# Attention scores by half-array matmuls, q loaded in long rows, and a new planned order

## The chip, the cores and the metric

The kernel runs on one core of a Trainium2 chip. The metric is the device time of one execution in microseconds (us). The core has five engines that run side by side and wait for one another through semaphores: TensorE (PE in the profile; PEld is its weight load), VectorE (DVE), ScalarE (ACT), GpSimd (POOL) and SyncE (SP), which here issues all transfers between HBM and the on-chip memory SBUF. Matmul results go to PSUM, which PE, DVE and ACT reach.

## The reference, cut to what matters

```python
# q, k, v: (2, 8, 576, 64), fp32
scores = scale * np.matmul(q, k.transpose(0, 1, 3, 2))
mask = (rel >= 0) & (rel < 64)             # rel = query position - key position
attn = softmax(np.where(mask, scores, -1e9))
x = (attn @ v) as (1152, 512)
# first expert layer
h = x @ w_in                               # 512 -> 2048
g = np.maximum(h, 0.0) + np.log1p(np.exp(-np.abs(h)))
x = g @ w_out                              # 2048 -> 512
# second expert layer: four experts, each token a weighted sum of all
p = domain_probs / (domain_probs.sum(-1, keepdims=True) + 1e-09)
out = sum over e of p[:, e] * (np.maximum(x @ w1[e], 0.0) @ w2[e])
```

## The kernel before, in words

**Attention.** The 1152 tokens are cut into 18 groups of 64 queries; because of the window of 64, a group sees 128 keys. Heads go in four pairs (NP = 4): 128 SBUF partitions hold the 64 dimensions of the one head and of the other. Three groups form a chunk, whose keys (kT), queries (qz) and values come by transfers from SP (`load_qk`, `load_v`). The score matmul (`scores_pe`, L957 to L962) takes the two heads of a pair in one go: qz holds, for each pair, 128 columns, the first 64 with the first head's queries in the upper 64 rows and zeros below, the last 64 with the second head's queries in the lower rows and zeros above. So a matmul over all 128 rows adds only zeros from the other head. The zeros are written once by DVE (`zeros`, L1022) into two qz buffers; the loads then fill the other halves with two transfers for each chunk (L858), in runs of 64 floats.

The rest of a group: DVE adds the mask and takes the row maximum (L968), ACT takes the exponentials and their sums (L972), DVE the reciprocals (`one_over`, L976 and L977), one of the engines scales the probabilities (L980 or L984), PE transposes them (L989), a copy brings them to SBUF (pT, L249 or L253), PE multiplies with v (L1001, on half of the output columns at a time), and two operations write x as a high and a low part (L249 or L253, then L1013).

**First expert layer.** 16 chunks of 128 hidden columns, in four units of four, over three blocks of 384 tokens: 48 steps. A step is twelve matmuls into h (L468), the softplus on ACT, DVE and POOL (L487 to L505; l minus w; then g's high part and its low part, both through the helper lines L249, L253 and L268), and twelve matmuls that add to acc (L538). Weights come as 64-bit floats and are turned into a high and a low fp32 part by a chain on ACT and DVE (`convert`, L391 to L415).

**Second expert layer.** Two pairs of token halves (2 x 320 and 2 x 256), 16 weight quads each: seven half products a quad (L703), sums (L724), relu in two parts (L768, L772), and the second matmuls (L798). The weight sums S and the token sums T run through L268.

**What sets the order.** Nothing is written out by hand. Each operation is an `Op` with a duration for each engine that may do it, what it comes after, and a due time. `plan()` (L177) works the due times back from the matmul steps, then goes through modelled time: it takes the operation that can start earliest, among those the most urgent, and picks its engine. The letters `E_...` in `P` (L50) list the engines that may do an operation: A is ACT, D is DVE, V is DVE when it shares SBUF ports with POOL, G is POOL. Letters ending in 0 hold for the first unit or the first block of tokens: E_T copies pT, E_H writes x's high part, E_P scales, E_R rounds in the softplus, E_S subtracts w from l, E_G and E_L make g's high and low part, E_S2 and E_T2 make the sums S and T. `PE` and `PE2` (L76) model a matmul; WB, DW2 and DV shift the due times of weight conversions and loads.

Of the kernel before, what the change touches and what calls it, by code (L numbers as in the profile page):

```python
# [21 lines left out]
def kernel(  # L22
# [124 lines left out]
    class Ring:  # L147
# [10 lines left out]
        def take(self, first):  # L158
# [519 lines left out]
    def quad(n, p, e, j, due1, due2):  # L678
# [162 lines left out]
    mask = ap_.tile([128, 2, 128], F32, bufs=1, name="mask")  # L841
    qz = [ap_.tile([128, GPC, NP, 2, W], F32, bufs=1, name=f"qz{i}") for i in range(2)]
    pn = cp.tile([128, NT // 128, E], F32, name="pn")
    psum = cp.tile([128, NT // 128], F32, name="psum")

    kT, vt = {}, {}
    qk_there, v_there = {}, {}
    qk_done, v_done = {}, {}

    def load_qk(c, due):  # L850
        b, s = c // CPB, (c % CPB) * CH

        def keys(k0, k1):
            if c not in kT:
                kT[c] = ap_.tile([128, NP, W + CH], F32, tag="kT", bufs=2, name=f"kT{c}")
            nc.sync.dma_start(out=kT[c][:, :, k0:k1], in_=k[b, :, :, s - W + k0:s - W + k1].rearrange("h p s -> p h s"))

        def queries(j, g0, g1):  # L858
            rows = slice(j * D, (j + 1) * D)
            nc.sync.dma_start(out=qz[c % 2][rows, g0:g1, :, j, :], in_=q[b, rows, s // W + g0:s // W + g1])  # L860


        if s:
            parts = [(0, W + CH, 0, GPC)]
        elif b:
            parts = [(W, W + CH, 0, GPC)]
        else:
            parts = [(W, 3 * W, 0, 1), (3 * W, W + CH, 1, GPC)]
        qk_there[c], after = [], rings["kT"].next()
        for k0, k1, g0, g1 in parts:  # L870
            there = [Op({"Q": ((k1 - k0) * 0.0057, lambda k0=k0, k1=k1: keys(k0, k1))}, after, due, 2.2)]
            if g0 == 0:
                qk_done[c], after = rings["kT"].take(there[0]), []
            for j in range(2):
                there.append(Op({"Q": ((g1 - g0) * 0.364, lambda j=j, g0=g0, g1=g1: queries(j, g0, g1))},
                                [qk_done[c - 2]] if c >= 2 else (), due, 2.2))
            for g in range(g0, g1):
                qk_there[c].append(there + qk_there[c][g0 - 1] if g0 else there)
# [18 lines left out]
    class Group:  # L897
# [59 lines left out]
        def scores_pe(self):  # L957
            k0 = W * self.il if self.i else W
            self.s = self.bank(0, [128, NP, 128])
            for hp in range(NP):  # L960
                nc.tensor.matmul(self.s[:, hp, :], lhsT=qz[self.c % 2][:, self.il, hp],  # L961
                                 rhs=kT[self.c][:, hp, k0:k0 + 128], start=True, stop=True)  # L962

# [57 lines left out]

    def zeros(i):  # L1022
        for j in range(2):
            nc.vector.memset(qz[i][(1 - j) * D:(2 - j) * D, :, :, j, :], 0.0)

    def masks():
# [108 lines left out]
    for n, (p, e, j) in enumerate(quads):  # L1135
# [60 lines left out]
```

## Time and profile before

| | us |
|---|---|
| median of 3 runs | 670.98 (670.78 to 674.19) |
| the profiled execution | 672.12 |
| its span, first to last instruction | 670.3 |
| PE busy, of the span | 633.2 (94%) |
| DVE busy | 502.9 (75%) |
| ACT busy | 353.1 (53%) |
| POOL busy | 296.2 (44%) |

The profile gives for each instruction its engine, source line, start and duration, and infers what ended each wait. Lines are those of the kernel file; helper lines (L249, L253, L268) are shared by many operations, which the tile's name tells apart. The busy rows in slices are tenths of a slice of 1/40 of the span. Matmuls are pipelined, so a busy PE need not be at its best pace. Durations in groups are means over all instructions of a group.

### The profile page before, as it was taken

To read this page: it belongs to the slowest core of one execution; us is meant where nothing else is said; L and a number is where in the kernel's file an instruction comes from. 1 tells how busy PE (TensorE), PEld (TensorE's weight loads), DVE (VectorE), ACT (ScalarE), POOL (GpSimd) and SP (SyncE) were. 2 spreads that over 40 slices of the span, in tenths; PEclk is the share of its full clock that TensorE was granted. 3 is DMA by queue.
4 is the path that set the end of the run, shared out by engine and by line. 5 is a ranking of instruction groups with operands and counts; after the bars stand their busy time and mean duration, and the time that the engine had idled before them with its cause. 6 is when DMAs were issued, how large, how long until landed. Compare 5 with 4: busy or idle time off the path is not lost.

```text
span 670.3 us, 10414 instructions
## 1 busy us (share of the span) xinstructions
PE 633.2 (94%) x3864; PEld 581.8 (87%) x3864; DVE 502.9 (75%) x902; ACT 353.1 (53%) x767; POOL 296.2 (44%) x281
## 2 busy tenths in 40 slices
PE   5668999999999899799999999999998999999997
PEld 5558999989999799688989998998887889888996
DVE  5998999999999978965666474564897685766643
ACT  5998987767677576434235243332534343434330
POOL 2222623334444386564716345181745536454310
PEclk9898999999999999899999999999999999999999
DMA  8995312311112321012211321231152132223001
GB/s 233 279 252 189 119 47 81 118 73 63 65 64 66 123 64 64 0 64 75 115 64 64 117 72 64 75 114 63 64 189 79 65 126 95 95 73 116 1 1 63
DMA packets 38946, 62.81 MB, mean 94 GB/s; under 512 B 12144, under 2 KB 15216, under 8 KB 38896
## 3 DMA queue, kind: packets, MB, share of 16 engines
q1 hardware_dynamic: 38896, 62.16, 28.9%
q8 instruction: 30, 0.49, 0.3%
q14 instruction: 20, 0.16, 0.1%
HBM read 59.79 MB, written 2.36 MB: 93 GB/s over the span
## 4 chain that ended last, share of the span: by engine, by line
PE 68%; DVE 21%; ACT 4%; issue 3%; DMA 2%; POOL 1%; SPq 1%; ACTq 0%; DVEq 0%; POOLq 0%
PE acc L798 27%; PE y L703 11%; PE z L703 7%; PE x L703 7%; PE acc L538 7%; PE h L468 6%; DVE g L268 2%; PE s L961 2%; DVE w L499 2%; DMA qz<-in_q_dram 2%; DVE km L412 2%; DVE G L772 1%; DVE l L505 1%; DVE xo L268 1%; DVE kh L406 1%
## 5 line engine op out<-in xcount | busy, mean ns | idle before, releaser
L798 PE MATMUL acc<-wb,G 128*128 128x512 f32 x864 | 211.0, 392 | 3.2 <-DVE G L772 3.2
L798 PEld LDWEIGHTS acc<-wb,G 128*128 128x128 f32 x864 | 158.2, 188 | 33.8 <-DVE G L772 4.6
L538 PE MATMUL acc<-g,w 128*128 128x384 f32 x576 | 112.9, 343 | 6.3 <-DVE g L268 5.0
L268 POOL TENSOR_TENSOR l<-l,w 128x384 f32<-128x384 f32 x48 | 68.1, 1424 | 110.2 <-DVE l L505 82.5
L538 PEld LDWEIGHTS acc<-g,w 128*128 128x128 f32 x576 | 101.3, 191 | 9.5 <-DVE g L268 7.4
L468 PE MATMUL h<-x,w 128*128 128x384 f32 x576 | 106.9, 336 | 2.2 <-DVE w L415 1.4
L468 PEld LDWEIGHTS h<-x,w 128*128 128x128 f32 x576 | 99.9, 188 | 3.6 <-DVE w L415 1.7
L268 POOL TENSOR_TENSOR wc<-S,wc 128x1024 fp32r<-128x1024 f32 x16 | 38.8, 2428 | 115.4 <-ACT wc L249 115.3
L768 ACT ACTIVATE G<-C 128x320 fp32r<-128x320 f32 (+3 forms) x64 | 35.9, 561 | 78.3 <-PE acc L798 39.6
L772 DVE SCALAR_TENSOR_TENSOR G<-C,G 128x320 fp32r<-128x320 f32 (+3 forms) x64 | 51.9, 812 | 32.1 <-ACT G L768 31.9
L703 PE MATMUL z<-xo,wc 128*128 128x320 f32 (+1 forms) x384 | 62.2, 297 | 1.5 <-DVE C L724 1.1
L703 PE MATMUL y<-xo,wc 128*128 128x320 f32 (+1 forms) x384 | 63.0, 300 | 0.1
L703 PE MATMUL x<-xo,wa 128*128 128x320 f32 (+1 forms) x384 | 61.6, 296 | 0.8 <-ACT p L249 0.5
L268 POOL TENSOR_TENSOR S<-rq 128x256 f32<-128x256 f32 x64 | 55.0, 866 | 13.9 <-DVE wc L268 8.5
L703 PEld LDWEIGHTS x<-xo,wa 128*128 128x128 f32 x384 | 56.2, 189 | 3.5 <-ACT p L249 0.8
L249 ACT ACTIVATE wa<-rq 128x512 fp32r<-128x512 f32 x64 | 31.1, 516 | 53.3 <-PE y L703 53.2
L703 PEld LDWEIGHTS y<-xo,wc 128*128 128x128 f32 x384 | 56.2, 192 | 2.7 <-DVE q L724 0.7
L703 PEld LDWEIGHTS z<-xo,wc 128*128 128x128 f32 x384 | 54.8, 190 | 2.2 <-DVE C L724 1.3
L268 POOL TENSOR_TENSOR wa<-rq,wa 128x256 fp32r<-128x256 f32 (+1 forms) x25 | 31.6, 1270 | 56.0 <-ACT wa L249 53.4
L249 ACT ACTIVATE wc<-S 128x1024 fp32r<-128x1024 f32 x32 | 33.7, 1052 | 32.2 <-PE z L703 30.3
L268 DVE TENSOR_TENSOR wb<-rq,wb 128x1024 fp32r<-128x1024 f32 x27 | 36.1, 1337 | 6.3 <-ACT wb L249 5.0
L249 ACT ACTIVATE wb<-rq 128x1024 fp32r<-128x1024 f32 x32 | 33.5, 1047 | 13.8 <-PE acc L798 13.8
(83 smaller groups left out, 986.2 us busy)
## 6 DMA issues: line engine op xcount, KB each, us to landing
rq<-in_moe_w_dram SPq DMA_DIRECT2D x64, 512.0 KB, 4.1
r<-in_moe_w_in_dram SPq DMA_DIRECT2D x16, 512.0 KB, 3.6
r<-in_moe_w_out_dram SPq DMA_DIRECT2D x16, 512.0 KB, 4.5
v<-in_v_dram SPq DMA_DIRECT2D x16, 256.0 KB, 6.0
out_dram<-tot SPq DMA_DIRECT2D x9, 256.0 KB, 2.0
kT<-in_k_dram SPq DMA_DIRECT2D x4, 512.0 KB, 4.8
qz<-in_q_dram SPq DMA_DIRECT2D x10, 192.0 KB, 7.5
kT<-in_k_dram SPq DMA_DIRECT2D x1, 384.0 KB, 8.2
```

The lines of the kernel that those rows point to most:

```text
L249: nc.scalar.activation(out, in_, AF.Copy)
L268: engine.tensor_tensor(out, in0, in1, op=op)
L406: nc.vector.scalar_tensor_tensor(h, word(1), 0xc0000000, h, op0=ALU.bitwise_and, op1=ALU.bitwise_or)
L412: nc.vector.scalar_tensor_tensor(f32(env["m"]), word(0), 2.0 ** -32, env["m"], op0=ALU.mult, op1=ALU.add)
L468: nc.tensor.matmul(h, lhsT=a[:, wi, kc, :], rhs=x[:, xi, kc, :], start=n == 0, stop=n == 3 * KC - 1)
L499: nc.vector.scalar_tensor_tensor(env["w"], env["w"], 1.0, env["e"], op0=ALU.subtract, op1=ALU.subtract)
L538: nc.tensor.matmul(acc[:, :BLK[blk]], lhsT=b[:, wi, i * 128:(i + 1) * 128], rhs=g[:, gi, :], start=start, stop=stop)
L703: nc.tensor.matmul(env[bank], lhsT=w[:, a, wi, kc * 128:(kc + 1) * 128], rhs=b[xi][:, kc, :], start=first and m == 0, stop=m == 5, skip_gr ...
L768: nc.scalar.activation(env["g", c][:, HI, a:a + w], of[what](), AF.Relu)
L772: nc.vector.scalar_tensor_tensor(g[:, LO, a:a + w], of[what](), 0.0, f32(g[:, HI, a:a + w]), op0=ALU.max, op1=ALU.subtract)
L798: nc.tensor.matmul(acc, lhsT=g[:, gi, i * 128:(i + 1) * 128], rhs=b[:, wi, :], start=j == 0 and m == 0, stop=j == QPE - 1 and m == 5)
L961: nc.tensor.matmul(self.s[:, hp, :], lhsT=qz[self.c % 2][:, self.il, hp], rhs=kT[self.c][:, hp, k0:k0 + 128], start=True, stop=True)
```

## The change

The queries of a chunk are loaded into a tile qT without zeros, one transfer for both heads of a pair, in rows of up to 768 floats. The score matmul is split by head: the upper 64 rows give output partitions 0 to 63, the lower 64 rows give partitions 64 to 127. The zero-writing and its dependencies go. In the planner one duration now serves all matmuls (a constant of 0.0133 us for each), a group's scores count 1.0 us in place of 0.87, the reciprocals count as sharing ports with POOL, three due-time shifts differ (WB, DW2, DV), and ten engine lists differ.

```diff
-        T0=32.94, ..., W0=-5.56, WB=3.07, SECOND=5.66, SLACK=-0.89,
+        T0=32.94, ..., W0=-5.56, WB=1.27, SECOND=5.66, SLACK=-0.89,
...
-        MERGED=1, FUS=(4, 4, 4, 4), WIDE=0, AHEAD1=2, DW2=36.0, DV=3.14, DQ=13.62, DW=23.71,
-
-        E_W1="A", E_W2="A", E_S2="G", E_T2="V", E_G="A", E_F="A", E_X="AV", E_T="A", E_H="A", E_R="A", E_S="G", E_L="VG", E_P="AG",
-        E_T0="AD", E_H0="AD", E_P0="AG", E_W0="AG", E_R0="AV", E_G0="AV", E_S0="G", E_L0="VG")
+        MERGED=1, FUS=(4, 4, 4, 4), WIDE=0, AHEAD1=2, DW2=33.65, DV=3.24, DQ=13.62, DW=23.71,
+
+        E_W1="A", E_W2="A", E_S2="VG", E_T2="VG", E_G="A", E_F="A", E_X="AV", E_T="A", E_H="AD", E_R="A", E_S="VG", E_L="V", E_P="AG",
+        E_T0="A", E_H0="A", E_P0="AVG", E_W0="AG", E_R0="A", E_G0="A", E_S0="G", E_L0="VG")
...
-    PE = lambda n: n / 2400 + 0.0026
-    PE2 = lambda n: n / 2400 + 0.0133
+    PE = lambda n: n / 2400 + 0.0133
...
-    qz = [ap_.tile([128, GPC, NP, 2, W], F32, bufs=1, name=f"qz{i}") for i in range(2)]
...
-        def queries(j, g0, g1):
-            rows = slice(j * D, (j + 1) * D)
-            nc.sync.dma_start(out=qz[c % 2][rows, g0:g1, :, j, :], in_=q[b, rows, s // W + g0:s // W + g1])
+        def queries(g0, g1):
+            if c not in qT:
+                qT[c] = ap_.tile([128, GPC, NP, W], F32, tag="qT", bufs=2, name=f"qT{c}")
+            nc.sync.dma_start(out=qT[c][:, g0:g1], in_=q[b, :, s // W + g0:s // W + g1])
...
-            for j in range(2):
-                there.append(Op({"Q": ((g1 - g0) * 0.364, lambda j=j, g0=g0, g1=g1: queries(j, g0, g1))},
-                                [qk_done[c - 2]] if c >= 2 else (), due, 2.2))
+            there.append(Op({"Q": ((g1 - g0) * 0.36, lambda g0=g0, g1=g1: queries(g0, g1))},
+                            [qk_done[c - 2]] if c >= 2 else (), due, 2.2))
...
-            o, s_done = self.on_pe(0, 0.87, self.scores_pe, [*qk_there[self.c][self.il], zeroed[self.c % 2], constant])
+            o, s_done = self.on_pe(0, 1.0, self.scores_pe, [*qk_there[self.c][self.il], constant])
...
-            o = Op({"D": (0.3, self.one_over)}, exps)
+            o = Op({"V": (0.3, self.one_over)}, exps)
...
-                nc.tensor.matmul(self.s[:, hp, :], lhsT=qz[self.c % 2][:, self.il, hp],
-                                 rhs=kT[self.c][:, hp, k0:k0 + 128], start=True, stop=True)
+                for j in range(2):
+                    half = slice(j * D, (j + 1) * D)
+                    nc.tensor.matmul(self.s[half, hp, :], lhsT=qT[self.c][half, self.il, hp, :],
+                                     rhs=kT[self.c][half, hp, k0:k0 + 128], start=True, stop=True)
...
-    def zeros(i):
-        for j in range(2):
-            nc.vector.memset(qz[i][(1 - j) * D:(2 - j) * D, :, :, j, :], 0.0)
...
-    zeroed = [Op({"D": (1.63, lambda i=i: zeros(i))}, due=-9.0 + i) for i in range(2)]
...
-        t += 42 * PE2(PAIRS[p][1])
+        t += 42 * PE(PAIRS[p][1])
```

More of the change, by code (lines that the diff above doesn't have):

```diff
@@ L51 @@
         BLK=(384, 384, 384),
-        T0=32.94, ATT=1.39, SD=(0.53, -2, 4.08, 0.35, 1.94, 4.92, 5.76, 0, 0, 0, 0, 0), AL=(-5.77, 13.49), AH=(-1.0, -8), W0=-5.56, WB=3.07, SECOND=5.66, SLACK=-0.89,
+        T0=32.94, ATT=1.39, SD=(0.53, -2, 4.08, 0.35, 1.94, 4.92, 5.76, 0, 0, 0, 0, 0), AL=(-5.77, 13.49), AH=(-1.0, -8), W0=-5.56, WB=1.27, SECOND=5.66, SLACK=-0.89,
         WL=(30, 5.08, 28.9), WH=(2.15, 1.15, 4.82),
-        MERGED=1, FUS=(4, 4, 4, 4), WIDE=0, AHEAD1=2, DW2=36.0, DV=3.14, DQ=13.62, DW=23.71,
-        E_W1="A", E_W2="A", E_S2="G", E_T2="V", E_G="A", E_F="A", E_X="AV", E_T="A", E_H="A", E_R="A", E_S="G", E_L="VG", E_P="AG",
-        E_T0="AD", E_H0="AD", E_P0="AG", E_W0="AG", E_R0="AV", E_G0="AV", E_S0="G", E_L0="VG")
+        MERGED=1, FUS=(4, 4, 4, 4), WIDE=0, AHEAD1=2, DW2=33.65, DV=3.24, DQ=13.62, DW=23.71,
+        E_W1="A", E_W2="A", E_S2="VG", E_T2="VG", E_G="A", E_F="A", E_X="AV", E_T="A", E_H="AD", E_R="A", E_S="VG", E_L="V", E_P="AG",
+        E_T0="A", E_H0="A", E_P0="AVG", E_W0="AG", E_R0="A", E_G0="A", E_S0="G", E_L0="VG")
     BLK = P.BLK
@@ L163 @@
     rings = {t: Ring(n) for t, n in dict(acc=4, h=2, a0=1, a1=1, G=3, g=GB, e=2, l=2, w=2, kh=2, ke=1, km=2, raw=RAW,
-                                         we=EARLY, wl=LATE, p=3, pT=2, kT=2, v=5, qz=2).items()}
+                                         we=EARLY, wl=LATE, p=3, pT=2, kT=2, v=5).items()}
     taken = [0]
@@ L685, in quad @@
         env = {}
-        dur = 6 * PE2(N)
+        dur = 6 * PE(N)
         A = {1: (0, 0), 2: (0, 1), 4: (0, 2), 5: (2, 0), 6: (2, 1), 7: (2, 2), 3: (2, 3)}
@@ L786, in quad @@
         n_acc = 2 * N // 128
-        dur2 = 6 * PE2(DM)
+        dur2 = 6 * PE(DM)
         def second(i):
@@ L841 @@
     mask = ap_.tile([128, 2, 128], F32, bufs=1, name="mask")
-    qz = [ap_.tile([128, GPC, NP, 2, W], F32, bufs=1, name=f"qz{i}") for i in range(2)]
     pn = cp.tile([128, NT // 128, E], F32, name="pn")
     psum = cp.tile([128, NT // 128], F32, name="psum")
-    kT, vt = {}, {}
+    kT, qT, vt = {}, {}, {}
     qk_there, v_there = {}, {}
@@ L1063 @@
         due_q.append(t)
-        t += 42 * PE2(PAIRS[p][1])
+        t += 42 * PE(PAIRS[p][1])
         if n:
-            t += 6 * PE2(DM) * (2 * PAIRS[quads[n - 1][0]][1] // 128)
+            t += 6 * PE(DM) * (2 * PAIRS[quads[n - 1][0]][1] // 128)
     due_q += [t, t]
@@ L1140 @@
             right_operands(p)
-        d2 = due_q[n + 1] + (42 * PE2(PAIRS[quads[n + 1][0]][1]) if n + 1 < len(quads) else 0.0)
+        d2 = due_q[n + 1] + (42 * PE(PAIRS[quads[n + 1][0]][1]) if n + 1 < len(quads) else 0.0)
         quad(n, p, e, j, due_q[n], d2)
```

## The prediction

> **What bounds the kernel now.** I read the page first: engine shares, then the 40 slices.
>
> ```profile
> span 670.3 us, 10414 instructions
> PE 633.2 (94%) x3864; PEld 581.8 (87%) x3864; DVE 502.9 (75%) x902; ACT 353.1 (53%) x767; POOL 296.2 (44%) x281
> PE   5668999999999899799999999999998999999997
> PEclk9898999999999999899999999999999999999999
> ```
>
> TensorE (PE) is full from the fourth slice on, so from about 50 us the kernel is bound by the two expert layers' matmuls, which the change does not touch in number. What can be won lies in the first three slices, where PE is at 5 or 6 tenths, and in the few slices under 9 later. The next view is the busy time in stretches of 5 us: after start:end and length stand the busy us and instruction counts of PE, PE's weight loads, DVE, ACT and POOL, then the granted clock, the DMA share and GB/s.
>
> ```profile
> 5.00:10.00 5.00, 4.38 (x21) 4.12 (x21) 1.44 (x13) 1.86 (x9) 0.00 (x0) 1.00 1.08 225
> 10.00:15.00 5.00, 3.52 (x27) 3.26 (x27) 2.80 (x21) 3.85 (x19) 1.79 (x5) 1.00 1.07 317
> 15.00:20.00 5.00, 3.56 (x60) 2.95 (x59) 4.83 (x32) 4.91 (x20) 1.45 (x4) 1.00 1.17 262
> 20.00:25.00 5.00, 4.03 (x41) 3.38 (x37) 3.75 (x17) 4.47 (x17) 0.63 (x1) 0.68 1.13 272
> 25.00:30.00 5.00, 3.89 (x42) 3.34 (x40) 4.93 (x19) 3.90 (x16) 2.27 (x4) 0.98 1.11 310
> 30.00:35.00 5.00, 2.84 (x44) 2.44 (x44) 4.88 (x22) 5.00 (x17) 1.64 (x3) 1.00 0.97 340
> 45.00:50.00 5.00, 2.39 (x27) 1.76 (x25) 4.96 (x15) 4.72 (x14) 1.37 (x1) 0.91 1.15 256
> 50.00:55.00 5.00, 4.94 (x32) 4.73 (x33) 3.85 (x10) 3.58 (x12) 0.00 (x0) 0.50 0.96 323
> ```
>
> Three things are full at once. The DMA share is at or above 1 up to 50 us. VectorE (DVE) and ScalarE (ACT) are full from 30 us on, and both have holes before: between 10 and 30 us ACT works 17.1 of 20 us and DVE 16.3. POOL is nearly empty. From 50 to 55 us PE works at half clock. The DMA view of the first 50 us says what the queue is filled with, and the timeline of PE what its lateness costs.
>
> ```profile
> DMA packets 16045, 12.76 MB, mean 255 GB/s; under 512 B 10512, under 2 KB 13584, under 8 KB 16041
> q1 hardware_dynamic: 16041, 12.71, 99.1%
> kT<-in_k_dram SPq DMA_DIRECT2D x4, 512.0 KB, 4.8
> qz<-in_q_dram SPq DMA_DIRECT2D x10, 192.0 KB, 7.5
> ...
> 4.60 2.05 PE L961 MATMUL s<-kT,qz 128*128 128x128 f32 x8 [4.60 <-DMA qz<-in_q_dram]
> 12.49 1.13 PE L961 MATMUL s<-kT,qz 128*128 128x128 f32 x8 [1.48 <-DMA qz<-in_q_dram]
> 21.90 2.08 PE L961 MATMUL s<-kT,qz 128*128 128x128 f32 x8 [0.97 <-DMA qz<-in_q_dram]
> ```
>
> A q transfer of 192 KB lands after 7.5 us, a k transfer of 512 KB after 4.8. The q tile holds runs of 64 floats (256 B) between the zeros, so the 2304 KB of q (2 x 8 x 576 x 64 floats) make 9216 of the 10512 short packets: 57% of all packets, 18% of the bytes. Each time a new chunk of 192 queries starts, the score matmul waits for q.
>
> **The change part by part.** *q in long rows.* A chunk's queries become one transfer of 128 rows with 3 x 4 x 64 floats (3072 B) each: 14 issues become 7, and some 9216 packets about 768. Of the 49.6 us that the queue is taken, q has between 18% (8.9 us, by bytes) and 57% (28 us, by packets); a k transfer carries 512 KB in 4.8 us, so q would go in a fraction of it. The queue then has room before 50 us and q stops being the last arrival. What is late next is not the queue but ACT and DVE. For the sum I therefore don't take DMA time but the holes that the lateness made. The first scores start at 4.60 us behind three issues, of which one q issue goes: I take 0.8 us. Between 10 and 30 us ACT is idle for 2.9 us, and the waits for q of 1.48 and 0.97 us stand ahead of it; I take the 2.9 us whole. Bounds for both together: 0 (everything after 30 us takes as long as its engines anyway and the order wastes it) and 7.0 us (ACT's hole of 3.1 us from 5 to 10 us, 2.9 us and 1 us more). Sum so far -3.7 us.
>
> *Zeros gone.* Four memsets leave DVE.
>
> ```profile
> L1024 DVE MEMSET qz<- 64x768 f32 x4 | 2.8, 698 | 1.6 <-PEq L1164 1.0 <-issue 0.6
> 6.81 0.29 DVE L968 CUSTOM_DVE_ANT_0 p<-s,mask 128x128 f32<-128x128 f32 x1 [2.45 <-PE s L961]
> ```
>
> They end well ahead of DVE's first real work at 6.81 us, which waits for PE: 0. Without that cover they would cost 2.8 us.
>
> *Scores by halves.* Eight instructions for a group (four matmuls in two passes) become sixteen, each with 64 rows, 64 output partitions and still 128 columns.
>
> ```profile
> 57.06 0.89 PE s L961 x8
> 72.14 0.61 PE o L1001 x16
> 72.75 1.09 PE s L961 x8
> 75.96 0.44 PE p L989 x4
> ```
>
> The trace has no such matmul. The nearest row is the value matmul: also sixteen instructions on half the output partitions, with 64 columns, 0.61 us. From below, 0.61 us again, if two halves run side by side; from above, the pace of the transposes, 0.11 us for 128 columns: sixteen one after another take 1.76 us. Twice the columns of the value row would be 1.22 us, less what the separate rows let overlap; I take 1.1 us, no change from 1.09. Only groups that run while PE is full count, about six after 50 us: bounds 6 x (0.61 - 1.09) = -2.9 and 6 x (1.76 - 1.09) = +4.0 us.
>
> The chain shows a score behind matmuls of the full array at 0.89 us and one behind the half-array value matmul at 1.09 us. The Trainium skill ("TensorEngine Tiling (Array Packing)", Tiling Modes) says that a change of tiling mode drains TensorE, which fits these 0.20 us; the same page (The Solution) makes the array four independent 64x64 tiles, which would bring the score to the lower bound. By the first rule alone two more drains where a score does not follow values, at 0.2 us and six groups, add at most 2.4 us; by the second 2.9 us go.
>
> *Engine letters of block 0.* Copies of the transposed probabilities (E_T0) and of the outputs to x (E_H0) lose DVE and go to ACT; the scaling by 1/sum (E_P0) may now go to DVE.
>
> ```profile
> L253 DVE COPY pT<-p 128x512 f32<-128x512 f32 x2 | 1.4, 688 | 1.8 <-PE p L989 1.8
> L253 DVE CAST x<-o 128x256 fp32r<-128x256 f32 x4 | 1.7, 419 | 0.0
> L249 ACT ACTIVATE pT<-p 128x512 f32<-128x512 f32 x16 | 9.4, 589 | 3.4 <-PE p L989 3.3
> L249 ACT ACTIVATE x<-o 128x256 fp32r<-128x256 f32 x14 | 5.3, 379 | 2.6 <-PE o L1001 2.3
> L984 ACT ACTIVATE p<-p,m 128x128 f32<-128x128 f32 x46 | 16.3, 392 | 0.6 <-DVE m L977 0.4
> ```
>
> DVE loses 3.1 us, ACT gains 2 x 0.589 + 4 x 0.379 = 2.7 us. A scaling on DVE has no row; the mask operation on the same 128x128 takes 0.29 us, so 3.1 us hold some ten, which take 10 x 0.392 = 3.9 us from ACT. Between +2.7 (none moves) and -1.2 us; with both engines full I take 0.
>
> *The half clock.* The 4.94 us that PE works at clock 0.50 are worth half, 2.5 us. If the first steps of the expert layer come closer together the clock stays up; it can as well go down elsewhere. I take -1.5 us, bounds -2.5 and +2.5.
>
> *Expert layers.* Now the later stretches and the groups from 165 to 270 us.
>
> ```profile
> 160.00:200.00 40.00, 39.77 (x229) 39.22 (x228) 38.65 (x59) 28.45 (x55) 18.16 (x13) 1.00 0.22 80
> 200.00:240.00 40.00, 37.33 (x212) 36.24 (x211) 38.16 (x51) 26.95 (x54) 18.82 (x17) 1.00 0.25 79
> 240.00:260.00 20.00, 20.00 (x117) 20.00 (x116) 15.17 (x24) 12.79 (x28) 14.53 (x15) 1.00 0.17 53
> 260.00:280.00 20.00, 15.84 (x91) 14.73 (x89) 19.68 (x25) 13.09 (x26) 14.44 (x11) 1.00 0.14 54
> 480.00:520.00 40.00, 37.47 (x218) 32.01 (x217) 33.06 (x49) 16.84 (x29) 23.27 (x22) 1.00 0.34 112
> ...
> L268 POOL TENSOR_TENSOR l<-l,w 128x384 f32<-128x384 f32 x25 | 34.5, 1387 | 41.7 <-DVE l L505 34.2 <-DVE w L499 5.0 <-PE h L468 2.6
> L268 POOL TENSOR_TENSOR g<-l,g 128x384 fp32r<-128x384 f32 x8 | 9.8, 1231 | 4.9 <-ACT g L249 4.5 <-PE acc L538 0.4
> L268 DVE TENSOR_TENSOR g<-l,g 128x384 fp32r<-128x384 f32 x16 | 14.1, 883 | 1.5 <-ACT g L249 1.5
> L505 DVE SCALAR_TENSOR_TENSOR l<-h,l 128x384 f32<-128x384 f32 x26 | 14.2, 547 | 5.2 <-ACT l L502 5.2
> ```
>
> E_L puts the low half of g on DVE alone, E_S lets DVE take l-w. On DVE such an operation takes about the 0.547 us of the row that reads one operand from PSUM, so each move shortens the softplus chain by 0.7 to 0.8 us. PE's holes there are 2.67 us from 200 to 240 us: -1.0, bounds 0 and -2.7. At the seam of the layers (260 to 280 us, hole 4.16) and of the two token pairs (480 to 520, hole 2.53) E_T2 and E_S2 let POOL and DVE share sums that one of them did alone: -2.0 together, bounds +2 (a slow POOL sum on the chain) and -6.7. The matmul constant of 0.0133 us, DV, WB and DW2 move due times, thus order only; they are in these bounds.
>
> The row of g on DVE averages 0.883 us against 0.547 us for the one that leaves the second SBUF operand alone: DVE waits while POOL works. The Trainium skill ("GPSIMD Engine Reference", Specifications) says that POOL shares its SBUF interfaces with VectorE and contends with instructions of two SBUF inputs; by it, what moves to DVE gives back waiting of other DVE work, which the sum leaves out.
>
> **Sum.** -3.7 - 1.5 - 1.0 - 2.0 = -8.2 us. The profiled execution took 672.1 us around its span of 670.3; that is 1.1 us above the median of 671.0. So 663.9 beside the profiled one and 662.8 beside the median: 663 us.
>
> **The rivals.** *Hidden anyway.* ACT, with the 2.7 us of copies that DVE gives up, has just the work that fills its 2.9 us of holes; the start gains only the 0.8 us, the clock stays as it is, and the other terms give a third. For it: ACT and DVE are full from 30 us. Against it: POOL and the scaling are free to move. -0.8 - 1.0 = -1.8: 669 us.
>
> *DVE becomes the bound of the first expert layer.* In 160 to 260 us DVE works 92.0 of 100 us. If all 25 l-w and 8 low halves come to it at 0.547 us, that is 18.1 us for 8.0 us of room, and PE, which needs g, waits 10.1 us; with the start's -3.7 the time is 671 + 6.4 = 677 us. It decides once more than 8.0 us net come in. Against it: the waiting of the 16 g on POOL, 16 x (0.883 - 0.547) = 5.4 us, would come back.
>
> *Nearly all holes close.* Start -7.0, clock -2.5, seams and layers -6: 655 us. For it, the queue's relief is far larger than any hole; against it, DVE and ACT at their limit to 50 us.
>
> *The halves don't overlap.* Scores at 1.76 us take 4.0 us of the gain: 667 us.
>
> **How the numbers follow.** Forecast 663 (658 to 667): 0.48. Hidden 669: 0.20. DVE bound 677: 0.13. Holes close 655: 0.10. No overlap 667: 0.09. The range reaches from the third rival's better side, 653, to 676, inside the DVE case; beyond lie some 2 in 10. A measurement tells about 0.5%, 3.4 us, from no change, so faster means under 667.6. The forecast, closed holes and most of no overlap: 0.66; the hidden case and the edges: 0.20; the DVE case and the edge beside it: 0.14.
>
> **What would show it.** Right: short packets in the first 50 us fall to some 1300, no wait of scores for q after the first, ACT above 18.5 us from 10 to 30 us, PE's full stretch about 4 us earlier, sixteen score instructions at about 1.1 us, no half clock near 50 us. Wrong: ACT just as holed with another releaser (pT or x), PE holes behind DVE g between 160 and 260 us, or scores near 1.8 us.

## The result, and the profile after

The changed kernel takes 654.22 us (median of 4 runs, 653.27 to 655.03); the kernel before, run beside it, takes 671.68 us (670.78 to 674.19). The ratio is 0.9734, 95% interval 0.9702 to 0.9765: 17.5 us faster, where 8.2 were forecast. The profiled execution took 654.69 us around a span of 652.6 us.

The page of the changed kernel, engine shares and two of the rows in slices:

```profile
span 652.6 us, 10673 instructions
PE 629.6 (96%) x4008; PEld 577.7 (89%) x4008; DVE 505.3 (77%) x1002; ACT 356.9 (55%) x778; POOL 192.6 (30%) x166
...
PE   7679999999999999999999999999999999999997
PEclk9999999999999999999999999999999999999999
```

The 7s and 8s that stood later in PE's row are gone, but for the 7 of the last slice, which both kernels have. DVE has the same busy time as before (502.9 us) with 100 instructions more; POOL has lost 104 us. The start first: the DMA view of the first 50 us, and PE's timeline (start, duration, then idle time before it and its releaser).

```profile
DMA packets 8093, 14.02 MB, mean 280 GB/s; under 512 B 1231, under 2 KB 4431, under 8 KB 8087
q1 hardware_dynamic: 8087, 13.95, 78.7%
...
qT<-in_q_dram SPq DMA_DIRECT2D x5, 384.0 KB, 6.3
```

```profile
4.14 1.97 PE L961 MATMUL s<-kT,qT 64*64 64x128 f32 x16 [4.14 <-DMA qT<-in_q_dram]
6.41 4.70 PE L961 MATMUL s<-kT,qT 64*64 64x128 f32 x48 [0.30 <-DMA qT<-in_q_dram]
...
13.90 1.09 PE L961 MATMUL s<-kT,qT 64*64 64x128 f32 x16
...
18.71 1.09 PE L961 MATMUL s<-kT,qT 64*64 64x128 f32 x16 [2.52 <-DMA qT<-in_q_dram]
```

Half the packets are gone and the queue is taken for 79% in place of 99%. Sixteen score matmuls take 1.09 us, as the eight did. The waits for q did not go: behind the first one two remain, 2.8 us together. The kernel before had three there, 3.1 us together: the two of 1.48 and 0.97 us, and this one of PE's timeline before:

```profile
7.27 3.75 PE L961 MATMUL s<-kT,qz 128*128 128x128 f32 x16 [0.62 <-DMA qz<-in_q_dram]
```

Next the busy time of the changed kernel in stretches (columns as in the prediction).

```profile
10.00:15.00 5.00, 5.00 (x76) 4.05 (x75) 4.63 (x38) 5.00 (x23) 1.17 (x4) 1.00 0.88 292
15.00:20.00 5.00, 2.48 (x44) 2.03 (x46) 3.92 (x21) 4.79 (x19) 0.00 (x0) 1.00 1.05 380
20.00:25.00 5.00, 3.91 (x72) 3.08 (x67) 4.42 (x20) 3.96 (x14) 2.32 (x2) 1.00 1.03 404
25.00:30.00 5.00, 3.24 (x40) 2.31 (x40) 4.63 (x19) 5.00 (x20) 1.44 (x4) 1.00 1.00 347
30.00:35.00 5.00, 4.16 (x38) 3.72 (x39) 4.00 (x17) 3.98 (x18) 0.72 (x2) 0.66 0.67 260
...
45.00:50.00 5.00, 3.07 (x32) 2.50 (x34) 5.00 (x14) 4.65 (x15) 1.27 (x1) 0.78 0.88 297
50.00:55.00 5.00, 5.00 (x34) 4.88 (x31) 4.77 (x13) 4.36 (x14) 1.74 (x3) 0.88 0.56 204
...
160.00:200.00 40.00, 40.00 (x233) 40.00 (x232) 40.00 (x67) 29.13 (x57) 4.86 (x4) 1.00 0.22 80
200.00:240.00 40.00, 40.00 (x233) 40.00 (x232) 39.77 (x64) 27.47 (x54) 17.03 (x11) 1.00 0.29 106
240.00:260.00 20.00, 19.43 (x111) 18.83 (x111) 17.43 (x34) 12.13 (x25) 2.89 (x2) 1.00 0.01 2
260.00:280.00 20.00, 18.91 (x115) 17.86 (x115) 17.80 (x28) 13.15 (x27) 13.77 (x10) 1.00 0.00 1
470.00:530.00 60.00, 59.95 (x374) 53.79 (x373) 45.95 (x87) 27.11 (x47) 22.61 (x17) 1.00 0.32 110
```

ACT works 18.75 us from 10 to 30 us (17.1 before). The reduced clock did not go, it moved and shrank: PE's busy time by what is missing in the clock, from 30 to 35 and 45 to 55 us, is 1.4 + 0.7 + 0.6 = 2.7 us; in the kernel before it is 1.4 us from 20 to 30, 0.2 from 45 to 50 and 2.5 from 50 to 55 us, 4.1 together. From 160 to 240 us PE has no hole at all, though DVE is full too. At the seam of the layers the hole is 1.09 us (4.16 before). At the change of token pairs PE now works 59.95 of 60 us. The same stretch of the kernel before, and three of its longest waits of PE behind the start (total us, times, longest):

```profile
470.00:530.00 60.00, 56.12 (x332) 48.76 (x331) 48.54 (x69) 26.91 (x50) 37.77 (x34) 1.00 0.32 110
```

```profile
PE acc L538 <- DVE g L268: 5.0, 3, 4.0
...
PE acc L798 <- DVE G L772: 3.2, 3, 1.7
...
PE h L468 <- DVE w L415: 1.4, 1, 1.4
```

and the waits of PE in the changed kernel that stand for the first and the last of these:

```profile
PE acc L537 <- DVE g L267: 1.6, 3, 1.0
...
PE h L467 <- ACT w L248: 0.2, 1, 0.2
```

**Where along the run the gain lies.** I counted the matmuls that each trace starts in each stretch of 5 us, weighted every kind by the planner's duration (n/2400 + 0.0133 us for n columns; small ones by their rows), and asked at what time each kernel has done the same share of the whole. The columns are moments of the changed kernel; the entries say how many us later (minus: earlier) the other kernel is at the same work. One profiled execution stands behind each row, some of them 1 to 3 us off their kernel's median (e15 the most), so differences under 2 us are not read.

| kernel (median us) | 100 | 190 | 240 | 285 | 460 | 530 | 630 |
|---|---|---|---|---|---|---|---|
| before (671.7) | -0.2 | 1.9 | 5.4 | 10.5 | 11.1 | 17.6 | 18.0 |
| e1 new scores, old plan (672.2) | -2.6 | 1.0 | 8.2 | 12.0 | 11.9 | 18.0 | 18.6 |
| e2 old scores, new plan (668.8) | 5.8 | 5.4 | 11.4 | 15.3 | 15.2 | 16.0 | 16.0 |
| e3 E_S, E_L back (665.3) | -3.9 | 2.7 | 4.6 | 11.6 | 12.4 | 12.7 | 12.5 |
| e4 E_S2, E_T2 back (652.5) | -2.7 | -2.4 | -1.9 | -2.4 | -2.3 | -0.1 | -1.4 |
| e5 q in short runs (657.3) | 2.1 | 2.1 | 2.2 | 2.2 | 2.6 | 2.9 | 3.1 |
| e6 e1 with E_S, E_L (667.7) | -3.4 | -3.6 | 0.6 | 4.9 | 4.8 | 11.0 | 11.9 |
| e7 WB, DW2, DV back (656.7) | -3.5 | -3.4 | -3.1 | -3.0 | -2.9 | -0.3 | 0.1 |
| e8 first layer's constant back (665.3) | 1.9 | 1.1 | 7.6 | 11.8 | 11.7 | 12.1 | 12.5 |
| e9 E_S2, E_T2, DW2 back (661.4) | -2.4 | -2.3 | -1.4 | -1.4 | -1.2 | 6.8 | 7.3 |
| e10 block 0's lists back (653.4) | -3.0 | -2.7 | -2.4 | -2.7 | -2.8 | -2.5 | -2.2 |
| e11 scores planned at 0.9 us (664.2) | -2.4 | -2.7 | 3.0 | 10.5 | 10.3 | 11.3 | 11.5 |
| e13 e11, low halves on DVE (656.2) | -0.9 | -1.5 | -0.9 | 2.2 | 2.4 | 3.2 | 1.7 |
| e15 before, low halves on DVE (663.2) | -0.9 | 1.2 | 3.5 | 4.2 | 4.2 | 5.9 | 5.0 |

In these executions the gain over the kernel before lies in three places, none of them the start: 3.5 us from 190 to 240 us, 5.1 us at the seam of the layers, 6.5 us at the change of token pairs (465 to 530 us; 5.1 us when the second layer's matmuls are counted one by one).

The column at 100 us needs care. e3, e4 and e7 have all instructions of the four engines in the order of the changed kernel to past 119 us, and still lie 2.7 to 3.9 us ahead of it there; e5 has its order to the end. What differs is the execution. Part of it is the granted clock, the third figure from the end of each row, here from 10 to 55 us in the changed kernel, in e3 and in e5:

```profile
10.00:55.00 45.00, 35.18 (x410) 29.24 (x408) 41.28 (x158) 41.74 (x145) 9.66 (x17) 0.92 0.78 278
```

```profile
10.00:55.00 45.00, 34.38 (x442) 28.57 (x442) 42.72 (x163) 44.19 (x153) 10.21 (x17) 1.00 0.77 278
```

```profile
10.00:55.00 45.00, 34.98 (x396) 28.29 (x394) 38.75 (x155) 39.81 (x138) 8.81 (x16) 0.85 0.87 273
```

e4 and e7 have 0.96. It isn't all: e9, of the same order to 223 us, has 0.89 and lies 2.4 us ahead. So starts that lie less than 4 us apart can't be ranked by this table, while the steps behind 100 us hardly vary where the order is the same (e5: 1.0 us from 100 to 630 us).

### The profile page after: what moved, and what is told of

Read it like the earlier page. It is cut to its first block, busy times and chain, and to the rows that moved or that the text cites. A ratio compares the mean times of both kernels' runs of the same rounds, so it can differ in the third digit from the quotient of the medians.

```text
span 652.6 us, 10673 instructions
## 1 busy us (share of the span) xinstructions
PE 629.6 (96%) x4008; PEld 577.7 (89%) x4008; DVE 505.3 (77%) x1002; ACT 356.9 (55%) x778; POOL 192.6 (30%) x166
## 4 chain that ended last, share of the span: by engine, by line
PE 60%; DVE 28%; ACT 6%; issue 3%; DMA 2%; SPq 0%; DVEq 0%; ACTq 0%
PE acc L797 28%; PE y L702 11%; PE z L702 7%; PE x L702 7%; DVE w L498 3%; DVE g L267 3%; DVE l L504 3%; PE acc L537 2%; DVE part L565 2%; DVE kh L405 2%; DVE km L411 2%; DVE l L267 2%; DMA qT<-in_q_dram 2%; DVE w L414 2%; ACT p L972 2%
## 5 line engine op out<-in xcount | busy, mean ns | idle before, releaser
L797 PE MATMUL acc<-wb,G 128*128 128x512 f32 x864 | 213.6, 392 | 0.0
L537 PE MATMUL acc<-g,w 128*128 128x384 f32 x576 | 110.9, 340 | 2.2 <-DVE g L267 1.6
L537 PEld LDWEIGHTS acc<-g,w 128*128 128x128 f32 x576 | 99.7, 188 | 5.9 <-DVE g L267 3.1
L267 POOL TENSOR_TENSOR wc<-S,wc 128x1024 fp32r<-128x1024 f32 x19 | 49.3, 2593 | 187.9 <-ACT wc L248 187.9
L767 ACT ACTIVATE G<-C 128x256 fp32r<-128x256 f32 (+2 forms) x64 | 35.8, 562 | 72.4 <-PE acc L797 50.2
L771 DVE SCALAR_TENSOR_TENSOR G<-C,G 128x256 fp32r<-128x256 f32 (+2 forms) x64 | 43.9, 686 | 30.2 <-ACT G L767 29.7
L267 POOL TENSOR_TENSOR l<-l,w 128x384 f32<-128x384 f32 x19 | 25.6, 1347 | 121.1 <-DVE l L504 100.7
L267 POOL TENSOR_TENSOR wa<-rq,wa 128x512 fp32r<-128x512 f32 (+1 forms) x32 | 38.8, 1220 | 26.4 <-ACT wa L248 22.8
L771 DVE SCALAR_TENSOR_TENSOR G<-x,G 128x320 fp32r<-128x320 f32 (+1 forms) x32 | 14.6, 457 | 34.2 <-ACT G L767 34.2
L767 ACT ACTIVATE G<-x 128x320 fp32r<-128x320 f32 (+1 forms) x32 | 13.1, 411 | 47.4 <-PE x L702 47.4
```

Source lines behind the costliest of these rows:

```text
L267: engine.tensor_tensor(out, in0, in1, op=op)
L537: nc.tensor.matmul(acc[:, :BLK[blk]], lhsT=b[:, wi, i * 128:(i + 1) * 128], rhs=g[:, gi, :], start=start, stop=stop)
L767: nc.scalar.activation(env["g", c][:, HI, a:a + w], of[what](), AF.Relu)
L771: nc.vector.scalar_tensor_tensor(g[:, LO, a:a + w], of[what](), 0.0, f32(g[:, HI, a:a + w]), op0=ALU.max, op1=ALU.subtract)
L797: nc.tensor.matmul(acc, lhsT=g[:, gi, i * 128:(i + 1) * 128], rhs=b[:, wi, :], start=j == 0 and m == 0, stop=j == QPE - 1 and m == 5)
```

## The experiments

All ratios are against the kernel before on the same chip. Since the experiments ran on several chips, differences between two of them are taken from their ratios, times 672 us; the whole change is 17.9 us by that count. e5 differs in how q lies in HBM.

### The two halves of the change alone

e1 is the kernel before with the new load and the half-array scores; lists, constants and due times stay.

```diff
-            nc.sync.dma_start(out=qz[c % 2][rows, g0:g1, :, j, :], in_=q[b, rows, s // W + g0:s // W + g1])
+            nc.sync.dma_start(out=qT[c][:, g0:g1], in_=q[b, :, s // W + g0:s // W + g1])
...
-            o, s_done = self.on_pe(0, 0.87, self.scores_pe, ...)
+            o, s_done = self.on_pe(0, 1.0, self.scores_pe, ...)
```

> The kernel before with the new q load and the score matmul by halves alone (no zeros, score duration 1.0 in the planner); engine lists, matmul constants and due shifts as before. Theory A (the gain of 17.5 us comes from the engine lists of the expert layers; the relief of the q transfers is hidden by DVE and ACT, which are full from 10 us on): 671, between 667 and 675. Theory B (the start pays, as the prediction had it, and the rest of the order only adds): 667 or less, with the gain standing by 50 us. Theory C (any edit re-deals the order by several us either way): anything between 660 and 680.

e2 is the opposite: all of the planner's edits, with the old zero-padded scores (0.87 us).

```diff
-    PE = lambda n: n / 2400 + 0.0026
-    PE2 = lambda n: n / 2400 + 0.0133
+    PE = lambda n: n / 2400 + 0.0133
+    PE2 = PE
...
-        E_S2="G", E_T2="V", ... E_S="G", E_L="VG", ...
+        E_S2="VG", E_T2="VG", ... E_S="VG", E_L="V", ...
```

> The kernel before with every planner edit of the change (engine lists, constants, due shifts, reciprocals as sharing ports), but q still in the zero-padded tile with 256-byte runs and the full-array score matmul. Theory A: most of the gain, 654 to 659. Theory B: 664 or more, since the queue is full again until 50 us. Theory C: no forecast closer than 655 to 675.

e1: 672.23 us, ratio 0.9979 (0.9961 to 0.9997). e2: 668.78 us, 0.9944 (0.9915 to 0.9972). Together they win 17.9 us, alone 1.4 and 3.8: the parts don't add. In the table e1 is 2.4 us ahead of the kernel before at 100 us, level at 190, and 2.8 behind at 240 us. The waits of PE in e1 from 150 to 290 us name the place:

```profile
PE acc L538 <- DVE g L268: 4.5, 3, 2.5
PE h L468 <- DVE l L505: 4.5, 4, 2.2
```

What the start may have gained is lost where the first expert layer waits for DVE's softplus. In e2 the start is 5.8 us behind the changed kernel (its profiled execution has a clock of 0.84 from 10 to 55 us) and another 10 us go between 190 and 285 us, although every planner edit but the score's duration is in it. The 654 to 659 us that one theory gave e2, because the lists carry the gain, was missed.

### Parts undone one at a time

Each of these is the changed kernel with one part as before.

```diff
e3
-        E_S="VG", E_L="V"
+        E_S="G", E_L="VG"
e4
-        E_S2="VG", E_T2="VG"
+        E_S2="G", E_T2="V"
e5
-            in_=q[b, :, s // W + g0:s // W + g1]
+            in_=q[b, s // W + g0:s // W + g1].rearrange("g h p w -> p g h w")
e7
-        WB=1.27, DW2=33.65, DV=3.24
+        WB=3.07, DW2=36.0, DV=3.14
e8 (h, acc of the first layer and its due times)
-        12 * PE(tb)
+        12 * (PE(tb) - 0.0107)
e10
-        E_H="AD", E_T0="A", E_H0="A", E_P0="AVG", E_R0="A", E_G0="A"
+        E_H="A", E_T0="AD", E_H0="AD", E_P0="AG", E_R0="AV", E_G0="AV"
```

> The changed kernel with l-w back on POOL alone and the low half of g on DVE or POOL (E_S=G, E_L=VG). Theory A: the 5 us that the changed kernel gains between 120 and 240 us, and part of the 5.5 us at the seam between the layers, are lost: 659 to 665, with PE holes behind DVE between 200 and 285 us again. Theory B: about 655, the lists of the first layer hardly matter, since DVE was as full as before.

> The changed kernel with the weight sums S on POOL alone and the token sums T on DVE alone (E_S2=G, E_T2=V). Theory A: the 6 us gained around the change of the token pairs (470 to 530 us) and part of the seam at 265 to 285 us are lost: 660 to 666; POOL busy rises by some 80 us. Theory B: about 655.

> The changed kernel, but q lies in HBM so that its one transfer for a chunk again consists of runs of 64 floats (256 bytes); tile, matmuls and planner as in the changed kernel. Theory A (with the new lists the first expert layer is bound by PE, so what the start loses is lost for good): PE 4 to 7 us later from 20 to 200 us, and 658 to 662 in all. Theory B (the start is hidden by DVE and ACT, full from 10 us on): within 2 us of the changed kernel, 653 to 656. If the first scores and not the queue made the difference, 656.

> The changed kernel with the three due shifts of before (WB 3.07, DW2 36.0, DV 3.14). Theory A (the 6 us at the change of the token pairs hang on when the second layer's weights are loaded and converted): 658 to 661, with PE waiting for DVE G or xo between 465 and 530 us. If the matmul constant made them: 653 to 656.

> The changed kernel with the first layer's matmuls at n/2400 + 0.0026 us in the planner again, 1152 x 0.0107 = 12.3 us too short in all, so that the second layer's due times lie 12.3 us too early. Theory A (due times only order what waits; the constant matters where the second layer's work meets the first's): 656 to 662, lost at the seam of the layers and at the change of the token pairs. Theory B: 653 to 656.

> The changed kernel with the lists of the first token block and first unit, and E_H, as before. Theory A (the start is set by the sum of DVE and ACT work, which the lists only shift): within 3 us of the changed kernel, 651 to 657, and the difference standing by 100 us. Theory B (the lists are what makes the queue's relief usable): 657 to 660.

| | us | ratio (95%) | cost of undoing, us |
|---|---|---|---|
| e3 first layer's lists | 665.27 | 0.9899 (0.9861 to 0.9936) | 11.1 |
| e4 second layer's lists | 652.49 | 0.9706 (0.9683 to 0.9729) | -1.9, not told apart |
| e5 short runs of q | 657.33 | 0.9782 (0.9742 to 0.9822) | 3.2, the intervals still touch |
| e7 due times | 656.67 | 0.9770 (0.9728 to 0.9812) | 2.4, not told apart |
| e8 matmul constant | 665.34 | 0.9895 (0.9860 to 0.9929) | 10.8 |
| e10 block 0's lists | 653.40 | 0.9731 (0.9682 to 0.9780) | -0.2, not told apart |

Two planner edits cost most when they are undone: the lists E_S and E_L (l minus w may go to DVE, g's low part to DVE alone), and the right matmul time for the first layer. Each undone costs 11 us, of 17.9 in all, so the parts don't add here either; below, an edit of no meaning of its own costs as much. e4 did not come to its 660 to 666 us, and e8 lies above its 656 to 662. In e3 the loss is spread from 100 us to the seam. In e8 it sits at 210 to 245 us and at the seam. e5 keeps a delay of 2 to 3 us from the start to the end: in this order a start that is late stays late. How much of that delay is the queue's is not shown, since executions of one order lie as far apart at 100 us and e5's had the lower clock; directly seen is that its transfers of 384 KB of q land after 7.4 us in place of 6.3.

### Parts taken together

e6 is e1 with the lists of the first layer; e9 the changed kernel with the second layer's lists and DW2 as before.

```diff
e6 (to e1)
-        E_S="G", E_L="VG"
+        E_S="VG", E_L="V"
e9 (to the changed kernel)
-        DW2=33.65 ... E_S2="VG", E_T2="VG"
+        DW2=36.0 ... E_S2="G", E_T2="V"
```

> The kernel before with the new q load and score matmul, and of the planner's edits only E_S=VG and E_L=V (l-w may go to DVE, the low half of g goes there always). Theory A (these two lists move the first layer's bound from DVE to PE, and the start's gain then stays): 657 to 664, PE without holes from 100 to 240 us, the 6 us at the change of the token pairs still lost. Theory C (lists help only in an order dealt with the right matmul constant): 667 or more.

> The changed kernel with S on POOL alone, T on DVE alone and the second layer's loads asked for at 36.0 us ahead again (E_S2=G, E_T2=V, DW2=36.0). Theory A (the two edits stand in for one another at the change of the token pairs: each alone cost 2 to 3 us there, together they cost the 6 us): 656 to 661 with 5 to 6 us lost between 465 and 530 us. If they are independent of it: 651 to 655.

e6: 667.65 us, 0.9941 (0.9920 to 0.9962): with the old constant the lists win 2.6 us in place of 11. e9: 661.37 us, 0.9841 (0.9790 to 0.9893). At the change of token pairs undoing the lists (e4) loses 2.2 us by the table, undoing the due times (e7) 2.6, lists and DW2 together 8.0. One covers for the other. With both undone PE's waits between 470 and 530 us are those of the kernel before again, one by one: 0.38, 0.35, 1.71, 1.19 and 0.17 us (0.39, 0.35, 1.71, 1.19 and 0.17). The trace of e9 (timeline of POOL, DVE and PE) shows what comes back there:

```profile
512.32 2.66 POOL L267 TENSOR_TENSOR wc<-S,wc 128x1024 fp32r<-128x1024 f32 x1 [4.23 <-ACT wc L248]
512.66 2.87 DVE L771 SCALAR_TENSOR_TENSOR G<-C,G 128x512 fp32r<-128x512 f32 x1
...
515.59 0.49 PE L797 MATMUL acc<-wb,G 128*128 128x512 f32 x1 [1.19 <-DVE G L771]
```

The kernel before has the same pair at 523 us, a POOL subtraction for a weight's low half of 2.66 us, G on DVE of 2.87 us that starts and ends just after it, and PE waiting for that. It has another at its layer seam (timeline of the kernel before):

```profile
277.61 2.34 POOL L268 TENSOR_TENSOR wb<-rq,wb 128x1024 fp32r<-128x1024 f32 x1 [0.55 <-ACT wb L249]
277.67 2.69 DVE L268 TENSOR_TENSOR g<-l,g 128x384 fp32r<-128x384 f32 x1
...
280.42 1.33 PE L538 MATMUL acc<-g,w 128*128 128x384 f32 x5 [3.96 <-DVE g L268]
```

A g of this size that meets no POOL operation takes 0.55 us on DVE.

### A nudge of the order

The planner's duration for the scores, alone, is set to 0.9 (e11) or 1.1 (e12) in place of 1.0. The lists and all other durations stay, so only the order and the choice of engines within the lists can differ.

```diff
-            o, s_done = self.on_pe(0, 1.0, self.scores_pe, ...)
+            o, s_done = self.on_pe(0, 0.9, self.scores_pe, ...)
```

> The changed kernel with 0.9 us in place of 1.0 for a group's scores in the planner, an edit of no meaning of its own (18 x 0.1 us). Theory C (the order is dealt anew by any edit, and part of the 17.5 us is a good deal): 655 to 666, with holes in other places. Theory A: 653 to 657.

> The same with 1.1 us, which is what the trace shows for the sixteen matmuls (1.09). Theory C: 655 to 666. Theory A: 653 to 657.

e11: 664.22 us, 0.9882 (0.9837 to 0.9926). e12: 654.03 us, 0.9729 (0.9690 to 0.9769). So 10 us hang on a tenth of a microsecond in a model, as much as on either of the two edits above: their 11 us may be the price of another order, and not of the edit itself. e11 loses 5.7 us from 190 to 240 us and 7.5 at the seam; its timeline at the first place, and the stretch of 5 us behind:

```profile
209.89 2.71 POOL L267 TENSOR_TENSOR wb<-rq,wb 128x1024 fp32r<-128x1024 f32 x1
...
210.27 2.75 DVE L267 TENSOR_TENSOR l<-l,w 128x384 f32<-128x384 f32 x1
...
213.62 0.44 PE L537 MATMUL acc<-g,w 128*128 128x384 f32 x1 [0.53 <-ACT g L248]
...
215.60 5.85 PE L537 MATMUL acc<-g,w 128*128 128x384 f32 x23 [1.53 <-DVE g L267]
```

```profile
215.00:220.00 5.00, 4.40 (x16) 4.40 (x17) 5.00 (x9) 2.11 (x4) 0.00 (x0) 0.66 0.02 7
```

An l minus w of 0.55 us takes 2.75 us beside a POOL subtraction of 2.71; PE waits twice, the granted clock falls to 0.66 and 23 matmuls take 5.85 us (24 take 4.32 us elsewhere in that trace): some 1.7 us that no hole shows. In e8 one of the long ones is another DVE operation, in the conversion of the first layer's weights (1.21 us elsewhere), beside the same kind on POOL:

```profile
212.37 2.51 POOL L267 TENSOR_TENSOR wb<-rq,wb 128x1024 fp32r<-128x1024 f32 x1 [1.36 <-ACT wb L248]
...
212.55 3.42 DVE L411 SCALAR_TENSOR_TENSOR km<-r,km 128x1024 f32<-128x1024 uint32 x1
```

Here PE waits for l, w and g from 218 to 228 us, 3.8 us in all.

### The suspected pair taken away

If these pairs make the slow orders slow, then an order without long POOL subtractions has to lose the loss. The low halves of the second layer's weights (wa, wb, wc) go to DVE alone, in e11's kernel (e13), the changed kernel (e14), the kernel before (e15) and e10's kernel (e16). The planner then makes a new order each time, so more differs than the place of these operations.

```diff
-            o2 = Op(tensors(n_el, lambda hi=hi, lo=lo, src=src: ..., ALU.subtract), [o1])
+            o2 = Op(tensors(n_el, lambda hi=hi, lo=lo, src=src: ..., ALU.subtract, "V"), [o1])
```

> The kernel with 0.9 us for the scores in the planner (664 us), and the low halves of the second layer's weights (wa, wb, wc: 32 to 54 operations of up to 1024 elements) on DVE alone. Theory D (the 10 us at the two spots between 190 and 285 us are POOL subtractions of 2.7 us that hold the SBUF port while a softplus operation of 0.55 us on DVE waits for it): 652 to 657, no DVE operation on l, w or g above 1.5 us between 200 and 285 us. Theory C (any edit re-deals, no one cause): no better forecast than 653 to 667.

> The changed kernel with the same edit. Theory D: within 3 us of the changed kernel, 651 to 657, since its order already has no such wait on the chain; DVE has room in the second layer (26 to 28 of 40 us). If DVE becomes the bound there: 658 or more.

> The kernel before with the same edit and nothing else. Theory D: the waits behind wa, wb and wc go, those of l-w on POOL itself (1.4 us each) stay: 662 to 668, the change of the token pairs (470 to 530 us) included. If POOL's port had no part in the 11 us: 669 to 673.

> The changed kernel with the first block's lists as before and the low halves on DVE alone, a version to beat both: 650 to 655 by theory D, 653 to 667 by theory C.

| | us | ratio (95%) |
|---|---|---|
| e13 from e11 (664.22) | 656.21 | 0.9750 (0.9719 to 0.9781) |
| e14 from the changed kernel (654.22) | 656.72 | 0.9758 (0.9726 to 0.9790) |
| e15 from the kernel before | 663.22 | 0.9866 (0.9832 to 0.9900) |
| e16 from e10 (653.40) | 657.10 | 0.9769 (0.9736 to 0.9802) |

The slow order gains 8.9 us, by the table in the two places where it had lost; e14 and e16 are 1.6 and 2.6 us slower than what they start from, not told apart. All three come out at 656 to 657 us; for e16 theory D had 650 to 655, and in e13 one g on DVE still takes 1.93 us, at 256 us. In the kernel before the same single argument wins 9.0 us (6.7 to 11.3), by the table at the seam (6 us) and at the change of pairs (5 us), with DVE busier (526.4 us against 502.9) and POOL less so (216.4 against 296.2). A new order comes with it, and e11 shows that a new order alone can move 10 us, so these runs make the pair's part in the loss likely without separating it from the order's:

```profile
PE 629.1 (96%) x3864; PEld 580.4 (88%) x3864; DVE 526.4 (80%) x950; ACT 353.5 (54%) x767; POOL 216.4 (33%) x233
```

### Two harmless edits at once

e17 is the changed kernel with e4's and e10's edits together, e18 is e12 with e4's.

```diff
e17
-        E_S2="VG", E_T2="VG", E_H="AD", E_T0="A", E_H0="A", E_P0="AVG", E_R0="A", E_G0="A"
+        E_S2="G", E_T2="V", E_H="A", E_T0="AD", E_H0="AD", E_P0="AG", E_R0="AV", E_G0="AV"
e18 (to e12)
-        E_S2="VG", E_T2="VG"
+        E_S2="G", E_T2="V"
```

> The changed kernel with the first block's lists as before, S on POOL alone and T on DVE alone. The start of e10 (2 us earlier than the changed kernel from 70 us on) and of e4 (2.5 us earlier) should not add, since both set the same DVE and ACT work: 650 to 653 if the order stays clear of long POOL operations on the softplus chain, 660 to 666 if it meets them (theory C and D together).

> The changed kernel with 1.1 us for the scores in the planner, S on POOL alone and T on DVE alone. 651 to 654, or 660 to 666 in the slow order, as for e17.

e17: 657.27 us, 0.9795 (0.9758 to 0.9831). e18: 656.14 us, 0.9785 (0.9753 to 0.9817). Edits that cost nothing measurable alone (e4, e10, e12) make it 4.1 and 3.4 us slower in these pairs, with intervals that just touch the changed kernel's; neither lies in one of its two expected ranges. None of the 18 kernels is told apart from the changed kernel on the better side; the best, e4, overlaps it.

## Why the prediction was right in its direction and wrong in its size

**The failed step** is the terms for the expert layers, -1.0, and for the two seams, -2.0 together. They measured -3.5, and -5.1 and -6.5. The prediction began with the claim that what can be won lies in the first three slices, and so took only a third of the holes it had quoted. Two things were left out. First, the holes did close nearly whole. Second, a hole is less than what a stall costs. For equal work the stretches to compare are 162 to 296 us and 472 to 547 us of the kernel before (quoted first; the middle row is the end of the first stretch) with 160 to 285 us and 460 to 530 us of the changed one:

```profile
162.10:296.36 134.26, 126.19 (x715) 122.85 (x715) 120.91 (x171) 83.92 (x165) 72.23 (x60) 0.99 0.20 68
280.00:296.00 16.00, 14.99 (x84) 14.48 (x85) 11.36 (x19) 4.20 (x9) 7.67 (x7) 0.89 0.17 65
471.55:546.75 75.20, 71.32 (x430) 62.45 (x428) 60.05 (x88) 32.61 (x60) 38.83 (x35) 1.00 0.30 103
```

```profile
160.00:285.00 125.00, 123.34 (x716) 121.39 (x715) 120.01 (x199) 83.32 (x163) 41.03 (x28) 1.00 0.19 68
460.00:530.00 70.00, 69.94 (x429) 62.80 (x428) 53.65 (x101) 33.03 (x61) 29.13 (x22) 1.00 0.32 110
```

Idle time of PE falls from 8.07 to 1.66 us and from 3.88 to 0.06, together 10.2 us. The stretches became 9.3 and 5.2 us shorter. Of the remaining 4 us, 1.6 lie in the clock of 0.89 behind the long wait of 3.96 us for g (14.99 x 0.11); where the others lie is open. Over the whole span PE's idle time (span less busy time, from the two pages) falls from 37.1 to 23.0 us, 14.1 of the 17.7 us between the spans; PE's busy time falls by the other 3.6, of which the mean clock of 0.994 in place of 0.990 makes some 2.5 (an estimate: 0.004 of its 630 us).

**What made the holes** stood in the prediction only as a note after the sum: g at 0.883 us on DVE against 0.547. That row ends at 270 us, ahead of the g of 2.69 us at the seam, and such a mean would have hidden it as well. The two rows of POOL's l minus w, before and after, show what freed DVE from it.

```profile
L268 POOL TENSOR_TENSOR l<-l,w 128x384 f32<-128x384 f32 x48 | 68.1, 1424 | 110.2 <-DVE l L505 82.5 <-DVE w L499 14.8 <-DVE m L976 10.3
```

```profile
L267 POOL TENSOR_TENSOR l<-l,w 128x384 f32<-128x384 f32 x19 | 25.6, 1347 | 121.1 <-DVE l L504 100.7 <-DVE m L976 10.1 <-DVE w L498 6.5
```

With 29 of these moved, and 100 DVE instructions more in all, DVE's total rose by only 2.4 us.

**The start**, -3.7 for q and -1.5 for the clock: the queue is relieved as said, but q went on being late (2.8 us of waits behind the first, 3.1 before), and its transfers did not go in a fraction of the 4.8 us of k: 384 KB land after 6.3 us. Two readings were too wide: only the first three of the six chunks wait for q, and the DMA share, said to be at or above 1 up to 50 us, is 0.68 from 40 to 45 us. In the two profiled executions the changed kernel is level with the one before at 100 us; as the same order ran 2.7 to 3.9 us earlier in e3, e4 and e7, the start is worth something between nothing and 4 us, and the runs don't settle how much. By e5 the long rows are worth some 3.2 us, but the intervals touch and its clock was lower. The clock's term, 4.1 us lost before and 2.7 after from 10 to 55 us, came to -1.4; with the clock of executions of one order between 0.89 and 1.00, that it came so near the forecast is luck.

**Scores by halves**: 1.1 us taken, 1.09 measured; neither lower nor upper bound. The rival that the halves don't overlap falls; what the Trainium skill has of four independent tiles ("TensorEngine Tiling (Array Packing)", The Solution), which would have brought 0.61 us, did not show either. **Zeros**, 0: nothing speaks against it. **Block 0's lists**, 0: right (e10), though ten scalings were to leave ACT for DVE and only eight run there, mostly from POOL, at 0.28 us each.

**The rivals.** *Hidden anyway*, at 669 us, happened in e1, in another place: not ACT takes the gain but the waits for DVE's softplus from 190 us on. *DVE becomes the bound* falls: DVE went from 92.0 to 97.2 of 100 us between 160 and 260 us, as the rival counted on, yet PE kept its pace: DVE does 165 instructions there in place of 134 and works only 5.2 us more, since with less on POOL its operations wait less (g's low part on DVE takes 0.641 us in the mean of 45 operations, 0.862 in the mean of 35 before). *Nearly all holes close*, 655 us, gave the time, but by another route, so its number is luck: the seams and layers brought 15 us against its 6, the start about 0 against its 7.

## What to carry to other kernels

Before costing a list that moves work between two engines, look in the timeline for single operations far above their group's median, and for what runs on the neighbour engine in that moment; a group's mean hides them, and the hole they leave on the bound engine is less than they cost. A planned order should be tried at two or three neighbouring values of its model before its gain is put down to an edit: here 0.1 us in one duration moved the time by 10 us, and two halves of a change were worth 1.4 and 3.8 us alone and 17.9 together. A gain at the start only counts if the stage behind it isn't waiting for something else, and two kernels' starts should be compared over several executions.

## What the runs showed of the hardware

An operation with two SBUF inputs on DVE that starts while POOL does one does not slow down by a share; in three of the pairs shown it ends about its own usual time after POOL's end: 0.55 us became 2.75 and 2.69 (0.4 us after POOL's end), 1.21 became 3.42 (1.1 us after). In the whole trace of the kernel before, all 18 g's on DVE that start inside a POOL operation, more than 0.1 us before its end, end 0.41 to 0.42 us after it. The 14 l's of L505 that do so, which read one operand from PSUM, take their usual 0.54 to 0.56 us. The nine kh's of L395 and L402 that do so, with one input of 1024 elements in SBUF, end 0.55 us after it, so the wait is not confined to two inputs. The Trainium skill ("GPSIMD Engine Reference", Specifications) says that the two share SBUF interfaces and contend where DVE has two SBUF inputs; the traces agree, and these numbers say by how much. It goes the other way too: in the changed kernel a sum on POOL, 0.87 us in the mean before, takes 4.27 us while DVE, which was at work when it started, goes on without a gap (timeline of POOL):

```profile
212.07 4.27 POOL L267 TENSOR_TENSOR S<-rq 128x256 f32<-128x256 f32 x1 [6.51 <-DVE w L414]
```

There the loser is POOL, and PE stays full. Which of the two starts first is decided by the order, and so by small numbers in the planner.

With q in runs of 256 B (e5; 14267 packets in the first 50 us against 8093) the same transfer of 384 KB lands after 7.4 us in place of 6.3; the whole kernel is 3.2 us slower, with intervals that still touch. The Trainium skill ("DMA: Bandwidth & Descriptors", Specifications) puts the smallest transfer for full rate at 512 B, which fits.
